# Where and when the sums of the second weight are made, and where the late weights lie

## The chip, the cores and the metric

The kernel runs on one core of one Trainium2 chip. The metric is the device time in microseconds (us) of one execution. The core has TensorE (PE; its weight loads are PEld), VectorE (DVE), ScalarE (ACT), GpSimd (POOL) and SyncE (SP), which issues the DMA transfers. Code runs on each engine in the order in which it is written; engines wait for each other through semaphores.

## The reference, cut to what matters

```
A  = softmax(q  @ k_lm^T * s)     # q, k, v: [4, 8, 576, 64]; 32 landmarks
Bm = softmax(q_lm @ k_lm^T * s);  C = softmax(q_lm @ k^T * s)
Z: six steps of Z = 2 Z - Z Bm Z
x  = (A Z C v) as tokens [2304, 512]
h  = x @ w_in;  x = (h * clip(h + 3, 0, 6) / 6) @ w_out    # FFN1, d_ff 2048
h  = x @ w_in2; g = where(h > 0, h, exp(min(h, 0)) - 1)
out = g @ w_out2                                            # FFN2, d_ff 2048
```

All data is fp32. A product on TensorE is made of pairs: each operand is split into a rounded part (hi) and the rest (lo), and three matmuls (hi hi, hi lo, lo hi) are summed. A cast on ACT makes hi, a subtraction on another engine makes lo (`to_pair`).

## The kernel before, in words

**FFN1** runs in 128 slots, 4 batches of 32. A slot has an h part (`slot_a1`) and, three slots later, the accumulation of x (`slot_a2`); the last of these are woven into FFN2's start (`late`, which the main loop takes through `tail`). Results go to DRAM as `x1d`.

**FFN2** has three tiles of 768 tokens (t = 0, 1, 2) of 8 quartets each, q = 0 to 23. A quartet (`quartet`) makes h for two d_ff blocks of 128 on each side of a seven-product form in place of eight products: seven blocks of 6 matmuls 128x384, with block sums on DVE (`a`, `u2`, `y`), then ELU on ACT and DVE (`gf`), its pair `gh`, `gl`, and one quartet later the second product (`second`, 36 matmuls 128x512 per quartet). Tile 2 (`WINO`) uses a seven-product form for the second product too (`wino2`, then `late2` for what is done after the last quartet). That form needs sums and differences of blocks of `w_out2`: `sums_out2(q)`, q = 0 to 7, reads two parts of `wo2d` (each 256 KB), makes four differences, their pairs, and stores them to `to2p` in DRAM.

**Buffers.** Tags with one buffer decide who waits. The tag `u` has three (`UB`), and is shared by the weight converters (`conv_out2`, `conv_in2`), the sums of `w_in2` in `load_in2`, the quartet's `u2`, and `sums_out2` (`scratch`; two of them, `raw` and `t`). `y` has two (`YB`). Second weights lie in four places (`w2_place`). FFN2's x of tiles 0 and 2 lies in 14 tiles `x20` to `x213` (`x_places`), that of tile 1 in the places that FFN1's weights left. `load_x(t)` loads four parts of x for each of two halves, makes seven sums of them (11 operations, with the pairs) and their casts on ACT; for tile 0 on DVE, for the others on POOL.

**Order.** The main program writes the work in the order of FFN1's slots, then of quartets with seven steps p each. `wanted(s)` gives what follows a place in time, by which the scheduler orders it on an engine against other work; `gated` holds work back to a slot. In FFN1's last batch, `sums` is stepped once a slot from slot 5 of the batch (`TSET`), and `run(sums)` does the rest before FFN2's loop. `load_x(1)` starts in q = 1 and `load_x(2)` in q = 9 (`XPACE`), a step for each p. In the last tile `late2` asks for late weight m + 3 when it starts on m, 12 of 512 KB in all:

```
if s == 0 and r % 2 == 0:
    for x in (2, 3) if m == 0 else (m + 3,):
        if x < NDEF * NQ // 2:
            load_late2(t, x)
```

Of the kernel before, what the change touches and what calls it, by code (L numbers as in the profile page):

```python
# [31 lines left out]
def nystrom_ffn_kernel(ctx: ExitStack, tc, q, k, v, w_in1, w_out1, w_in2, w_out2, out):  # L32
# [61 lines left out]
    NDEF = 3  # L94
    AHEAD = 4
# [6 lines left out]
    TSET, RUSH, LASTS = 5, 4, 4  # L102
# [272 lines left out]
    def sums_out2(q):  # L375

        raw = scratch(2, DM)
        for i in range(2):
            gated(sp.dma_start(out=raw[:, i], in_=wo2d[q + i * NQ]))
        yield  # L380
        t = scratch(4, HDM)
        (b21, b22), (b11, b12) = ((raw[:, i, 0:HDM], raw[:, i, HDM:]) for i in range(2))
        gated(sub(t[:, 0], b12, b11))
        gated(sub(t[:, 1], b22, t[:, 0]))
        gated(sub(t[:, 2], b22, b12))
        gated(sub(t[:, 3], t[:, 1], b21))
        yield
        h = raw.bitcast(F32R).rearrange("p a n -> p (a n)").rearrange("p (j n) -> p j n", j=4)
        gated(act.copy(out=h, in_=t))
        gated(sub(t.bitcast(F32R), t, h.bitcast(F32), pool))  # L390
        yield
        o = q % 2 * HDM
        for x, y in ((0, h.bitcast(F32)), (1, t)):
            sp.dma_start(out=to2p[:, q // 2, x, :, o:o + HDM].rearrange("j p n -> p j n"), in_=y)
        yield

    place = [0]
# [14 lines left out]
    def load_late2(t, m):  # L412

        j, r = (1, 2, 0)[m // (NQ // 2)], m % (NQ // 2)
        w = w2_place()
        sp.dma_start(out=w, in_=to2p[j, r].rearrange("x p n -> p x n"))
        wo2[t, "late", m] = w.bitcast(F32R)
# [561 lines left out]
    def load_x(t, eng):  # L979
# [3 lines left out]
        for kk in range(2):  # L983
# [7 lines left out]
            if t:  # L991
                f = [
                    nat.tile([128, G, HALF], F32, name="xf", tag=n).rearrange("p g t -> p (g t)")[:, 0:T2]
                    for n in ("ath0", "ath1", "atl0")
                ]
            else:
                f = [stg.tile([128, W], F32, name="xf", tag="y", bufs=YB)[:, 0:T2] for _ in range(2)]
                f.append(ft.tile([128, T2], F32, name="xf", tag="at", bufs=1))
# [175 lines left out]
    def late2(t):  # L1174
# [51 lines left out]
        for n in range(NDEF):  # L1226
# [6 lines left out]
            for r, s in order:  # L1233
# [6 lines left out]
                if s == 0 and r % 2 == 0:  # L1240
                    for x in (2, 3) if m == 0 else (m + 3,):
                        if x < NDEF * NQ // 2:
                            load_late2(t, x)
                if s == 0 and (n or r >= RUSH):
                    pair(n * NQ + r + AHEAD)
                w = wo2[t, "late", m]
                c = slice(r % 2 * HDM, r % 2 * HDM + HDM)
                for j, (g, y) in enumerate(terms(pairs[n * NQ + r], (w[:, 0, c], w[:, 1, c]))):
                    start = r == 0 and j == 0 and not (n == 0 and s == 1)
                    bmm(ps[s], g[:, tok(s)], y, start, r == NQ - 1 and j == 2 and not n == s == 0)  # L1250
                    yield
# [146 lines left out]
    def all_sums():  # L1398
        for q in range(NQ):
            yield from sums_out2(q)  # L1400

    sums = all_sums()
    for i in range(END, NA):
# [17 lines left out]
        if (i - END) % O2 == 0 and conv:  # L1421
# [3 lines left out]
            gate[0] = None  # L1425
            if not conv:
                wanted(i + 6)
                flush()
        if i >= NA - SB + TSET:
            gate[0] = marks["slot"]  # L1430
            wanted(i + 4)
            next(sums, None)
            gate[0] = None
# [23 lines left out]
    run(sums)  # L1457
# [3 lines left out]
    behind, tail, xs, n = seconds(), late(), x0, 0  # L1461
    for q in range(NTT * NQ):
# [3 lines left out]
        if q % NQ == XPACE and q // NQ + 1 < NTT:  # L1466
            xs = load_x(q // NQ + 1, pool)
        steps_ = quartet(q)
        for p in range(7):
# [5 lines left out]
            if p == 4 and q % NQ == NQ - 1 and q // NQ in WINO:  # L1475
                load_late2(q // NQ, 0)
                load_late2(q // NQ, 1)
            next(xs, None)
# [45 lines left out]
```

## Time and profile before

| | |
|---|---|
| median of 3 runs | 844.37 us (844.35 to 847.03) |
| profiled execution | 845.85 us |
| its span, first to last instruction | 844.1 us |
| its mean granted TensorE clock | 0.982 of full |
| PE, PEld busy | 786.1 (93%), 697.5 (83%) |
| DVE, ACT, POOL busy | 554.8 (66%), 463.6 (55%), 388.3 (46%) |
| DMA | 184.56 MB, mean 219 GB/s |

The profiled execution has 1.75 us around its span, and stands 1.48 over the median. FFN1 ends and FFN2 begins near 435 us; tile 1 begins near 580 and tile 2 near 707. A row of the trace gives start, duration, engine, line of the kernel, operation, out<-in by the program's names, size and count, and in square brackets the idle time just before it with what ended that. Because a helper records every operation, all rows carry the line L115; names and sizes tell operations apart. A busy PE in the trace isn't PE at its peak, so PE's clock is to be looked at with its busy time.

### The profile page before, as it was taken

To read this page: it belongs to the slowest core of one execution; us is meant where nothing else is said; L and a number is where in the kernel's file an instruction comes from. 1 tells how busy PE (TensorE), PEld (TensorE's weight loads), DVE (VectorE), ACT (ScalarE), POOL (GpSimd) and SP (SyncE) were. 2 spreads that over 40 slices of the span, in tenths; PEclk is the share of its full clock that TensorE was granted. 3 is DMA by queue.
4 is the path that set the end of the run, shared out by engine and by line. 5 is a ranking of instruction groups with operands and counts; after the bars stand their busy time and mean duration, and the time that the engine had idled before them with its cause. 6 is when DMAs were issued, how large, how long until landed. Compare 5 with 4: busy or idle time off the path is not lost.

```text
span 844.1 us, 16146 instructions
## 1 busy us (share of the span) xinstructions
PE 786.1 (93%) x5860; PEld 697.5 (83%) x5860; DVE 554.8 (66%) x1108; ACT 463.6 (55%) x1012; POOL 388.3 (46%) x383
## 2 busy tenths in 40 slices
PE   5699989999999999989993899999999999999988
PEld 3476777688878899889893799998888989999988
DVE  7898686567546654575675776655575545777774
ACT  3687545656566565664653565646544434565551
POOL 2576566557645565456667656331280000322311
PEclk9799999999999999999996999999999999999999
DMA  9966931885586546755876467686664465867455
GB/s 334 403 188 227 304 95 59 243 276 171 195 257 209 167 117 203 252 172 167 310 249 222 147 253 261 233 294 256 230 223 157 167 225 182 295 230 243 165 186 181
DMA packets 112623, 184.56 MB, mean 219 GB/s; under 512 B 8160, under 2 KB 66016, under 8 KB 112544
## 3 DMA queue, kind: packets, MB, share of 16 engines
q1 hardware_dynamic: 112544, 183.53, 64.6%
q8 instruction: 46, 0.75, 0.4%
q14 instruction: 33, 0.27, 0.1%
HBM read 130.02 MB, written 53.48 MB: 217 GB/s over the span
## 4 chain that ended last, share of the span: by engine, by line
PE 64%; DMA 11%; DVE 7%; issue 6%; POOL 6%; ACT 4%; SPq 1%; DVEq 0%; POOLq 0%; ACTq 0%
PE x L115 33%; PE h L115 26%; PE bk L115 5%; DMA u<-in_moe_w_out 3%; DVE u L115 2%; POOL gl L115 1%; DMA w<-to2p 1%; POOL x L115 1%; DMA out<-ob 1%; POOL y L115 1%; DMA wo2d<-y 1%; DMA kt<-in_k 1%; ACT u L115 1%; DMA to2p<-u 1%; DMA x<-x1d 1%
## 5 line engine op out<-in xcount | busy, mean ns | idle before, releaser
L115 PE MATMUL h<-x,wi 128*128 128x384 f32 x1008 | 206.9, 341 | 14.8 <-DVE u L115 13.2
L115 PEld LDWEIGHTS h<-x,wi 128*128 128x128 f32 x1008 | 180.1, 190 | 25.5 <-DVE u L115 14.2
L115 PE MATMUL x<-gh,wo 128*128 128x288 f32 (+1 forms) x896 | 198.8, 298 | 1.5 <-ACT xs L115 1.1
L115 PEld LDWEIGHTS x<-gh,wo 128*128 128x128 f32 x896 | 149.5, 189 | 12.1 <-issue 7.2
L115 PE MATMUL x<-gl,wo 128*128 128x288 f32 (+1 forms) x448 | 130.7, 295 | 0.6 <-POOL gl L115 0.6
L115 POOL TENSOR_TENSOR gl<-gf,gh 128x288 fp32r<-128x288 f32 (+1 forms) x100 | 85.7, 860 | 81.7 <-ACT gh L115 72.2
L115 ACT CAST gh<-gf 128x288 fp32r<-128x288 f32 (+2 forms) x160 | 72.6, 454 | 85.0 <-DVE gf L115 84.6
L115 PE MATMUL x<-w,gh 128*128 128x512 f32 (+1 forms) x420 | 114.3, 349 | 0.9 <-ACT gh L115 0.9
L115 PE MATMUL h<-atl,nh 128*128 128x288 f32 (+2 forms) x256 | 81.9, 320 | 8.6 <-DVE gf L115 5.4
L115 DVE SCALAR_TENSOR_TENSOR gf<-gf,y 128x384 f32<-128x384 f32 x80 | 59.9, 750 | 44.0 <-ACT gf L115 43.9
L115 PEld LDWEIGHTS x<-gl,wo 128*128 128x128 f32 x448 | 84.5, 189 | 2.2 <-POOL gl L115 1.1
L115 ACT ACTIVATE gf<-h,half_b 128x288 f32<-128x288 f32 (+2 forms) x128 | 63.9, 500 | 40.5 <-PE h L115 31.9
L115 POOL TENSOR_TENSOR x<-x,gf 128x384 f32<-128x384 f32 x16 | 18.2, 1158 | 145.8 <-PE x L115 86.9
L115 PE MATMUL x<-w,ghl 128*128 128x512 f32 (+1 forms) x378 | 83.9, 346 | 0.3 <-DMA w<-to2p 0.2
L115 PEld LDWEIGHTS x<-w,gh 128*128 128x128 f32 x420 | 75.3, 193 | 7.4 <-ACT gh L115 1.4
L115 DVE SCALAR_TENSOR_TENSOR gf<-gf,h 128x288 f32<-128x288 f32 (+1 forms) x112 | 49.5, 442 | 45.0 <-ACT gf L115 44.3
L115 PE MATMUL h<-ath,nl 128*128 128x288 f32 (+2 forms) x256 | 76.6, 299 | 0.0
L115 PE MATMUL h<-ath,nh 128*128 128x288 f32 (+2 forms) x256 | 76.3, 298 | 0.0
L115 PE MATMUL x<-w,gl 128*128 128x512 f32 (+1 forms) x210 | 73.6, 351 | 2.7 <-DVE gl L115 2.7
L115 ACT ACTIVATE gf<-y 128x384 f32<-128x384 f32 x80 | 42.0, 525 | 59.7 <-DVE y L115 59.7
L115 PEld LDWEIGHTS x<-w,ghl 128*128 128x128 f32 x378 | 62.1, 189 | 6.1 <-DVE ghl L115 0.4
L115 PEld LDWEIGHTS h<-atl,nh 128*128 128x128 f32 x256 | 48.4, 189 | 22.4 <-DVE gf L115 9.8
(171 smaller groups left out, 1462.1 us busy)
## 6 DMA issues: line engine op xcount, KB each, us to landing
wi<-wi2p SPq DMA_DIRECT2D x64, 448.0 KB, 5.2
wi2p<-wi SPq DMA_DIRECT2D x32, 448.0 KB, 3.1
u<-in_moe_w_in SPq DMA_DIRECT2D x25, 512.0 KB, 4.6
w1c<-w1d SPq DMA_DIRECT2D x48, 256.0 KB, 4.7
w<-wo2p SPq DMA_DIRECT2D x24, 512.0 KB, 6.3
ub<-in_moe_w_out SPq DMA_DIRECT2D x16, 512.0 KB, 10.3
u<-in_moe_w_out SPq DMA_DIRECT2D x16, 512.0 KB, 5.4
wo2p<-w SPq DMA_DIRECT2D x16, 512.0 KB, 4.0
```

Source lines behind the costliest of these rows:

```text
L115: inst = getattr(self.eng, name)(*a, **kw)
```

## The change

The sums of `w_out2` are no longer stepped in FFN1's last batch. A generator `more` steps them, one step for each p from quartet q = 8 on, so the 32 steps take q = 8 to 12. They no longer use `u`: each takes four of the x tiles `x20` to `x211`, which hold x of tile 0 before and x of tile 2 after (`spare_x`). Their four differences go from DVE to POOL; the cast of 128x1024 becomes two of 128x512, the subtraction for lo likewise, and two stores of 512 KB become four of 256 KB. Late weights 2 to 11 are loaded in halves into x tiles of tile 2, in the order in which these come free, and seven of them are asked for at m = 0; weights 0 and 1 stay in `w2_place`. x of tile 0 uses two `u` buffers where it used two `y` and one `at`. `load_x(2)` starts at q = 12 (`TX`).

```
--- before.py
+++ after.py
@@ -92,6 +92,8 @@
     WINO = (2,)
     HDM = DM // 2
     NDEF = 3
+    NLATE = 2
+    RUSH, LASTS, TX = 4, 4, 4
     AHEAD = 4
     T1 = 320
     YB, UB, SE = 2, 3, 1
@@ -99,7 +101,6 @@
     GATE1, O2, NEW1 = 8, 2, 0
     PACE, NEW, PACE1 = 0.5, -4, 0.2
     XSET, XPACE = 4, 1
-    TSET, RUSH, LASTS = 5, 4, 4
     NAT = 25, 28, 31
 
     strict = [False]
@@ -374,27 +375,28 @@
 
     def sums_out2(q):
 
-        raw = scratch(2, DM)
-        for i in range(2):
-            gated(sp.dma_start(out=raw[:, i], in_=wo2d[q + i * NQ]))
+        a, b, c, d = (spare_x(4 * q + i).rearrange("p (j n) -> p j n", j=2) for i in range(4))
+        for i, y in enumerate((b, a)):
+            sp.dma_start(out=y, in_=wo2d[q + i * NQ].rearrange("p (j n) -> p j n", j=2))
         yield
-        t = scratch(4, HDM)
-        (b21, b22), (b11, b12) = ((raw[:, i, 0:HDM], raw[:, i, HDM:]) for i in range(2))
-        gated(sub(t[:, 0], b12, b11))
-        gated(sub(t[:, 1], b22, t[:, 0]))
-        gated(sub(t[:, 2], b22, b12))
-        gated(sub(t[:, 3], t[:, 1], b21))
+        sub(c[:, 0], a[:, 1], a[:, 0], pool)
+        sub(c[:, 1], b[:, 1], c[:, 0], pool)
+        sub(d[:, 0], b[:, 1], a[:, 1], pool)
+        sub(d[:, 1], c[:, 1], b[:, 0], pool)
         yield
-        h = raw.bitcast(F32R).rearrange("p a n -> p (a n)").rearrange("p (j n) -> p j n", j=4)
-        gated(act.copy(out=h, in_=t))
-        gated(sub(t.bitcast(F32R), t, h.bitcast(F32), pool))
+        for x, y in ((a, c), (b, d)):
+            to_pair(y, x.bitcast(F32R), y.bitcast(F32R), pool)
         yield
         o = q % 2 * HDM
-        for x, y in ((0, h.bitcast(F32)), (1, t)):
-            sp.dma_start(out=to2p[:, q // 2, x, :, o:o + HDM].rearrange("j p n -> p j n"), in_=y)
+        for j, ys in enumerate(((a, c), (b, d))):
+            for x, y in enumerate(ys):
+                sp.dma_start(out=to2p[2 * j:2 * j + 2, q // 2, x, :, o:o + HDM].rearrange("j p n -> p j n"), in_=y)
         yield
 
-    place = [0]
+    def spare_x(i):
+        return xp[0].tile([128, 2, T2], F32, name="x2", tag=f"x2{i % 12}").rearrange("p a n -> p (a n)")[:, 0:2 * HDM]
+
+    place = [0, 0]
 
     def w2_place():
         place[0] += 1
@@ -412,9 +414,17 @@
     def load_late2(t, m):
 
         j, r = (1, 2, 0)[m // (NQ // 2)], m % (NQ // 2)
-        w = w2_place()
-        sp.dma_start(out=w, in_=to2p[j, r].rearrange("x p n -> p x n"))
-        wo2[t, "late", m] = w.bitcast(F32R)
+        if m < NLATE:
+            w = w2_place()
+            sp.dma_start(out=w, in_=to2p[j, r].rearrange("x p n -> p x n"))
+            wo2[t, "late", m] = [w[:, :, i * HDM:i * HDM + HDM].bitcast(F32R) for i in range(2)]
+            return
+        wo2[t, "late", m] = []
+        for i in range(2):
+            place[1] += 1
+            w = xp[0].tile([128, 2, T2], F32, name="x2", tag=f"x2{(place[1] - 1) % 14}")[:, :, 0:HDM]
+            sp.dma_start(out=w, in_=to2p[j, r, :, :, i * HDM:i * HDM + HDM].rearrange("x p n -> p x n"))
+            wo2[t, "late", m].append(w.bitcast(F32R))
 
     def load_out2(q):
 
@@ -994,8 +1004,8 @@
                     for n in ("ath0", "ath1", "atl0")
                 ]
             else:
-                f = [stg.tile([128, W], F32, name="xf", tag="y", bufs=YB)[:, 0:T2] for _ in range(2)]
-                f.append(ft.tile([128, T2], F32, name="xf", tag="at", bufs=1))
+                f = scratch(2, T2)
+                f = [f[:, 0], f[:, 1], scratch(1, T2)[:, 0]]
             for o, r, c in ((f[0], 0, 1), (l[0], 0, 0), (l[2], 1, 1), (l[1], 1, 0)):
                 sp.dma_start(out=o, in_=x1d[2 * r + kk, :, t0 + c * T2:t0 + c * T2 + T2])
             yield
@@ -1238,14 +1248,13 @@
                     if r == RUSH:
                         inline()
                 if s == 0 and r % 2 == 0:
-                    for x in (2, 3) if m == 0 else (m + 3,):
+                    for x in range(2, 9) if m == 0 else (m + 6,) if m > 2 else ():
                         if x < NDEF * NQ // 2:
                             load_late2(t, x)
                 if s == 0 and (n or r >= RUSH):
                     pair(n * NQ + r + AHEAD)
-                w = wo2[t, "late", m]
-                c = slice(r % 2 * HDM, r % 2 * HDM + HDM)
-                for j, (g, y) in enumerate(terms(pairs[n * NQ + r], (w[:, 0, c], w[:, 1, c]))):
+                w = wo2[t, "late", m][r % 2]
+                for j, (g, y) in enumerate(terms(pairs[n * NQ + r], (w[:, 0], w[:, 1]))):
                     start = r == 0 and j == 0 and not (n == 0 and s == 1)
                     bmm(ps[s], g[:, tok(s)], y, start, r == NQ - 1 and j == 2 and not n == s == 0)
                     yield
@@ -1395,11 +1404,6 @@
     newton(2)
     conv = [lambda kk=kk: conv_out2(kk) for kk in range(NKT)]
     conv += [lambda m=m, kk=kk: conv_in2(m, kk) for m in range(NQ) for kk in range(2)]
-    def all_sums():
-        for q in range(NQ):
-            yield from sums_out2(q)
-
-    sums = all_sums()
     for i in range(END, NA):
         b, r = i // SB, i % SB
 
@@ -1423,14 +1427,6 @@
             wanted(i + 4)
             conv.pop(0)()
             gate[0] = None
-            if not conv:
-                wanted(i + 6)
-                flush()
-        if i >= NA - SB + TSET:
-            gate[0] = marks["slot"]
-            wanted(i + 4)
-            next(sums, None)
-            gate[0] = None
         if i >= NA - SB + XSET:
             wanted(i + 4)
             next(x0, None)
@@ -1454,18 +1450,19 @@
         for q in range(NTT * NQ):
             yield from (wino2 if q // NQ in WINO else second)(q)
 
-    run(sums)
     flush()
     wanted(NA - 6)
     load_in2(1)
-    behind, tail, xs, n = seconds(), late(), x0, 0
+    behind, tail, xs, more, n = seconds(), late(), x0, iter(()), 0
     for q in range(NTT * NQ):
         wanted(NA + 4 * q - 2)
         if q:
             load_in2(q + 1) if q + 1 < NTT * NQ else None
-        if q % NQ == XPACE and q // NQ + 1 < NTT:
+        if q % NQ == (TX if q // NQ + 1 in WINO else XPACE) and q // NQ + 1 < NTT:
             xs = load_x(q // NQ + 1, pool)
         steps_ = quartet(q)
+        if q == (WINO[0] - 1) * NQ:
+            more = (None for r in range(NQ) for _ in sums_out2(r))
         for p in range(7):
             if p == 2:
                 load_out2(q)
@@ -1475,6 +1472,7 @@
             if p == 4 and q % NQ == NQ - 1 and q // NQ in WINO:
                 load_late2(q // NQ, 0)
                 load_late2(q // NQ, 1)
+            next(more, None)
             next(xs, None)
             wanted(NA + 4 * q + 4 * p / 7)
             next(steps_)
```

**DVE, where FFN1 ends and FFN2 begins.** `gf` and `gl` of 128x288 are FFN1's; `u<-u 128x256` are differences of the second weight; `u<-u,wi` and `u<-wi,u` are `load_in2(1)`'s sums; rows with `a_` are quartet 0's, `u<-h,a_` its `u2`. Before:

```order
L115 SCALAR_TENSOR_TENSOR gf<-gf,h 128x288
L115 TENSOR_TENSOR u<-u 128x256 x3
L115 TENSOR_TENSOR gl<-gf,gh 128x288
L115 TENSOR_TENSOR u<-u 128x256
L115 TENSOR_TENSOR y<-h,a_5917 128x384
L115 SCALAR_TENSOR_TENSOR gf<-gf,y 128x384
L115 TENSOR_TENSOR gl<-gf,gh 128x384
L115 TENSOR_TENSOR u<-u 128x256 x4
L115 TENSOR_TENSOR u<-u,wi 128x128 x2
L115 TENSOR_TENSOR u<-wi,u 128x128 x2
L115 TENSOR_TENSOR u<-h,a_5917 128x384
L115 TENSOR_TENSOR u<-u,wi 128x128
L115 TENSOR_TENSOR u_5919<-h,u 128x384
```

After the change:

```order
L116 TENSOR_TENSOR gl<-gf,gh 128x288
L116 SCALAR_TENSOR_TENSOR gf<-gf,h 128x288
L116 TENSOR_TENSOR gl<-gf,gh 128x288
L116 TENSOR_TENSOR u<-h,a_5819 128x384
L116 TENSOR_TENSOR y<-h,a_5819 128x384
L116 TENSOR_TENSOR u_5821<-h,u 128x384
L116 SCALAR_TENSOR_TENSOR gf<-gf,y 128x384
L116 TENSOR_TENSOR gl<-gf,gh 128x384
L116 TENSOR_TENSOR y<-h,u_5821 128x384
L116 TENSOR_TENSOR u<-h,u 128x384
L116 TENSOR_TENSOR y<-h,u_5821 128x384
L116 SCALAR_TENSOR_TENSOR gf<-gf,y 128x384
```

The eight differences of the second weight are gone, the sums of quartet 1's weight no longer stand here (two and two of them now stand 12 to 18 rows higher, between FFN1's `gf` and `gl`, and the others behind quartet 0's next rows), and quartet 0's `u2` stands ahead of its first `y`.

**ACT, in quartet 0 and at quartet 1's first block.** `COPY a_` opens quartet 1; `CAST x_` are casts of x of tile 1, `CAST gh` make the pair of quartet 0's ELU. Before:

```order
L115 CAST x_6403<-xf 128x384
L115 ACTIVATE gf<-gf 128x384
L115 ACTIVATE gf<-y 128x384
L115 COPY a_6115<-h 128x384
L115 CAST wi<-wi 128x384
L115 ACTIVATE gf<-gf 128x384
L115 CAST gh<-gf 128x384
```

After the change:

```order
L116 CAST gh<-gf 128x384
L116 ACTIVATE gf<-gf 128x384
L116 COPY a_6017<-h 128x384
L116 CAST x_6303<-xf 128x384
L116 ACTIVATE gf<-y 128x384
L116 CAST wi<-wi 128x384
L116 CAST gh<-gf 128x384
```

A cast of x of tile 1 stood ahead of `a` and the ELU's rows; it now stands between `a` and the second of the two `gh` casts.

**SP, the last weight loads.** `w_` are in `w2_place`, `x_` in x tiles, `to2p` are late weights, `wo2p` the last quartet's. Before:

```order
L115 DMA w_9626<-wo2p 128x2x512
L115 DMA w_9664<-to2p 128x2x512
L115 DMA w_9666<-to2p 128x2x512
L115 DMA w_9777<-to2p 128x2x512
L115 DMA w_9806<-to2p 128x2x512
L115 DMA w_9871<-to2p 128x2x512
L115 DMA out<-ob 128x256 x2
L115 DMA w_9779<-to2p 128x2x512
L115 DMA out<-ob 128x256
L115 DMA w_9899<-to2p 128x2x512
L115 DMA w_9936<-to2p 128x2x512
L115 DMA w_9963<-to2p 128x2x512
```

After the change:

```order
L116 DMA x_9823<-to2p 128x2x256
L116 DMA x_9837<-to2p 128x2x256
L116 DMA w_9672<-wo2p 128x2x512
L116 DMA x_9831<-to2p 128x2x256
L116 DMA x_9845<-to2p 128x2x256
L116 DMA x_9825<-to2p 128x2x256
L116 DMA x_9839<-to2p 128x2x256
L116 DMA x_9833<-to2p 128x2x256
L116 DMA x_9847<-to2p 128x2x256
L116 DMA x_9829<-to2p 128x2x256
L116 DMA x_9843<-to2p 128x2x256
L116 DMA w_9710<-to2p 128x2x512
```

Ten late halves now stand ahead of weight 0 (`w_9710`), where before weights 0 and 1 came first and each next one when a place came free.

## Rows read from the trace of the kernel before

**Rows 1.** Windows: span, busy us of each engine, clock, DMA share, GB/s

```profile
core 0: us, PE busy (x) PEld busy (x) DVE busy (x) ACT busy (x) POOL busy (x), PEclk, DMA share, GB/s
440.00:460.00 20.00, 6.25 (x30) 5.78 (x30) 10.16 (x21) 6.21 (x11) 15.46 (x12) 0.71 0.54 187
```

**Rows 2.** Chain that ended last, part of the join: start, us, what

```profile
446.41 2.69 DVE u L115 x3
...
454.00 2.18 POOL wi L115 x2
456.19 0.57 DVE u L115
```

**Rows 3.** Timeline of PE at the join: start, us, engine, what, idle before

```profile
435.23 1.21 PE L115 MATMUL h<-x,wi 128*128 128x384 f32 x6
436.28 0.29 PE L115 MATMUL x<-gh,wo 128*128 128x288 f32 x1
...
437.07 1.22 PE L115 MATMUL h<-x,wi 128*128 128x384 f32 x6
...
456.80 1.65 PE L115 MATMUL h<-x,wi 128*128 128x384 f32 x4 [12.91 <-DVE u L115]
...
472.38 0.79 PE L115 MATMUL x<-w,gl 128*128 128x512 f32 x1 [2.74 <-DVE gl L115]
...
483.88 1.23 PE L115 MATMUL h<-x,wi 128*128 128x384 f32 x6
484.94 0.62 PE L115 MATMUL x<-w,gh 128*128 128x512 f32 x2
...
486.31 0.87 PE L115 MATMUL h<-x,wi 128*128 128x384 f32 x4
```

**Rows 4.** Timelines of POOL and SP at the join

```profile
434.02 1.01 POOL L115 TENSOR_TENSOR xf<-xf,x 128x384 f32<-128x384 f32 x1 [0.64 <-PE h L115]
...
459.06 1.01 POOL L115 TENSOR_TENSOR xf<-xf,x 128x384 f32<-128x384 f32 x1
...
455.01 0.48 SPq L115 DMA_DIRECT2D xf<-x1d  x1
```

**Rows 5.** Timelines in FFN1's last slots: PE, POOL, DVE

```profile
379.70 0.40 PE L115 MATMUL h<-atl,nh 128*128 128x288 f32 x1 [1.40 <-DVE gf L115]
...
406.62 0.40 PE L115 MATMUL h<-atl,nh 128*128 128x288 f32 x1 [1.39 <-DVE gf L115]
...
402.67 2.38 POOL L115 TENSOR_TENSOR u<-u 128x1024 fp32r<-128x1024 f32 x1 [2.62 <-ACT u L115]
...
403.09 2.91 DVE L115 TENSOR_TENSOR u<-u,wi 128x128 f32<-128x128 f32 x2 [1.27 <-DMA u<-wi2d]
405.93 0.28 DVE L115 TENSOR_TENSOR u<-wi,u 128x128 f32<-128x128 f32 x1
```

**Rows 6.** Timeline of PE near the end

```profile
818.87 3.04 PE L115 MATMUL h<-w,ghl 128*128 128x256 f32 x18 [3.42 <-DMA w<-to2p]
...
823.63 0.45 PE L115 MATMUL x<-w,gh 128*128 128x256 f32 x2
...
827.99 3.40 PE L115 MATMUL x<-w,ghl 128*128 128x256 f32 x27
```

**Rows 7.** Groups of instructions by shape: count, busy us, mean ns, idle before

```profile
L115 POOL TENSOR_TENSOR gl<-gf,gh 128x256 fp32r<-128x256 f32 x16 | 12.0, 748 | 9.2 <-ACT gh L115 9.2
...
L115 POOL TENSOR_TENSOR wi<-u,wi 128x512 fp32r<-128x512 f32 x16 | 21.1, 1333 | 0.0
...
L115 POOL TENSOR_TENSOR x<-xf,x 128x384 fp32r<-128x384 f32 x16 | 18.4, 1160 | 0.0
...
L115 ACT CAST x<-xf 128x384 fp32r<-128x384 f32 x24 | 12.1, 511 | 13.0 <-POOL xf L115 8.4 <-DVE xf L115 4.4
```

**Rows 8.** Windows of tile 1: columns as in the first group

```profile
608.00:624.00 16.00, 15.68 (x78) 13.75 (x77) 10.07 (x13) 7.93 (x18) 13.43 (x13) 1.00 0.56 194
624.00:640.00 16.00, 15.28 (x76) 13.43 (x75) 11.13 (x18) 8.79 (x19) 10.31 (x9) 1.00 0.55 182
640.00:656.00 16.00, 16.00 (x81) 14.35 (x80) 8.45 (x16) 6.90 (x14) 0.00 (x0) 1.00 0.51 180
```

**Rows 9.** The page's DMA queues: packets, MB, share of 16 engines' span

```profile
q1 hardware_dynamic: 112544, 183.53, 64.6%
```

## The prediction, made before the changed kernel ran

> **What bounds the kernel now.** I read the time in windows first, then the chain of work that ended last, then TensorE's own instructions around every wait. PE is busy 93% of the span, so only places where PE stands still, or runs at the lower clock, are worth anything. In 440 to 460 us PE works 6.25 of 20 us at a mean granted clock of 0.71, while POOL is busy 15.46 [rows 1]. It is the largest gap of the trace, and it lies at the join of the two FFNs. The chain through it [rows 2] has no PE: DVE `u` work (2.69), later POOL `wi` (2.18), then DVE `u` again (0.57). The first are sums of the second weight (they hold two of the three `u` buffers), the last is quartet 0's own `u2`, which can only have a buffer when sums and the weight load of quartet 1 have given theirs back. PE's rows there show one wait of 12.91 on DVE `u` and one of 2.74 on `gl` [rows 3]. Two smaller places count: two stalls of 1.40 and 1.39 in FFN1's last slots [rows 5], and 3.42 at the very end, on a late weight from `to2p` [rows 6].
>
> **Term 1, the join.** From quartet 0's block 0 (435.23) to quartet 2's (483.88) is 48.65 us [rows 3]. The work in it at full speed: 14 h blocks of 1.05 (435.23 to 436.28), 36 FFN1 matmuls of 0.132 (six from 436.28 to 437.07) and 30 second matmuls of 0.228 (six from 484.94 to 486.31): 14.7 + 4.75 + 6.85 = 26.3. So 22.4 are lost now, in waits and in the lower clock behind them. The change takes all sums out of the `u` buffers here, so half of quartet 1's weight sums stand 14 rows ahead of quartet 0's `u2` on DVE in place of right before it, the other half behind it, and `u2` has its buffer at once; the row order of DVE at the join shows it. What is late next is x of tile 1, which stays where it was: its first half starts on POOL at 434.02 [rows 4]; 11 operations of 1.16 [rows 7] end at 446.8. The second half's load takes from SP 455.01 to POOL 459.06, 4.05 [rows 4], so 450.9, and its first POOL operation (1.01) ends at 451.9. On ACT, in the order after the change, a cast of `x` stands between quartet 0's two `gh` casts; cast, relu, `wi` cast, `gh` cast at about 0.51 each (the form 128x384) [rows 7] end at 453.9. PE would need that `gh` at 435.23 + 7.35 + 4.75 + 2.1 (two more blocks) + 0.7 (three second matmuls) = 450.1. That leaves 3.8 idle, and about 1.5 of lower clock behind it, taken from the late stage: 27 matmuls took 4.76 (818.87 to 823.63) behind a 3.42 wait where 27 take 3.24 normally (3.40 less the last one's tail) [rows 6]. 22.4 - 5.2 = **-17.2**. Bounds: -20.6 if the cast of x comes without idling PE for long, and -12.0 if waits of 10 us stay.
>
> **Term 2, FFN1's last slots.** The eight 128x1024 subtractions on POOL leave. At 402.67 one of 2.38 runs beside a pair of 128x128 subtractions on DVE that take 2.91 (two more of the kind take 0.28 each right behind them), and PE then waits 1.39 [rows 5]; the other wait, 1.40, stands behind such an operation too. I take both off: **-2.8**. Bounds: 0 (x of tile 0 now needs two `u` buffers, and may bring waits of its own) to -4.5 (the smaller ones go too).
>
> **Term 3, the late weights.** Ten of twelve now have a place of their own from the freed x tiles, and the first seven of these are asked for together, long before use. The 3.42 wait and 1.5 behind it [rows 6] go; I keep 0.6, as weights 0 and 1 are still asked for behind other loads on SP. **-4.3**; bounds -1.5 (a first weight is as late as now by half) to -5.3.
>
> **Term 4, the middle tile.** Eight sums in 32 steps, seven a quartet: 4.6 quartets. A quartet is 7 x 1.05 + 36 x 0.228 = 15.6 us by rows 3, so 72 us. POOL gets 8 x (4 subtractions of 128x256 at 0.75 + 2 of 128x512 at 1.33) = 45 us [rows 7], ACT 16 casts 128x512, some 0.65 each scaled from 0.51. POOL is idle there now and ACT 40% busy. But POOL's work isn't free for the others: in 608 to 640, where POOL makes x of tile 2 (13.43 + 10.31 = 23.7 us), PE was idle 0.32 + 0.72 = 1.04, and in 640 to 656, without POOL, not at all [rows 8]. In proportion, 45 x 1.04 / 23.7 = **+2.0**; bounds 0 (quartets have slack at every other place) to +5.8 (three times that, since the operations come in one order with the casts). x of tile 2 starts three quartets later and meets the last sums; its last cast still stands at quartet 15's start, one quartet ahead of use, so I cost it at nothing; without that cover it would cost some 5 us once.
>
> DMA moves the same bytes in smaller parts: 32 stores of 256 KB for 16 of 512 KB, and 20 late halves for 10 whole weights. SP issues 26 more, which the quartets' PE time hides as it hides the others; without that cover each would cost about what the 0.48 of SP's row is [rows 4], 12 us.
>
> **Sum.** -17.2 - 2.8 - 4.3 + 2.0 = -22.3. The profiled run took 845.85, so 823.5; it stood 1.48 over the median of 844.37, so I forecast **822.0** us.
>
> **The rivals.**
> *The join keeps more.* With the `u` wait gone, x of tile 1 or the load of quartet 1's weights is late by 10 us more than worked out: term 1 falls to about -7, 832 us. For it: POOL is at 15.46 of 20 us there [rows 1]; against it: 2 x 2.4 of that are sums that leave.
> *DMA fills up.* Sums read and write 12.6 MB in 72 us. 183.53 MB take 64.6% of 844.1 [rows 9], so 12.6 MB take 37 us, +0.52 on a share of 0.51 to 0.56 [rows 8]: full. Then weights of quartets 9 to 12 come late; they are asked for a quartet ahead, so I give +5, 827 us.
> *DVE is blocked by POOL.* If each DVE operation with two SBUF inputs, of which a quartet has 8, waited for a whole POOL operation (as the pair at 403.09 did [rows 5]), DVE would need 8.45 [rows 8] + 8 x 1.31 = 18.9 us for a quartet of 15.7: 3.2 x 4.6 = +15, 837 us in all. Against it: POOL is busy 62% of that stretch, not all, and an operation met at its middle costs half, so 8 x 0.62 x 0.65 = 3.3 us, 11.7 in all, under 15.7. The Trainium skill, "SBUF — State Buffer", section "Who interferes with whom", says that a DVE instruction with two SBUF inputs and a GpSimd instruction share a port pair which one of them locks until it is done; by that rule alone, with every operation hit, it is this rival. The trace agrees on the single case: 2.91 for two operations of 0.28 beside POOL's 2.38.
> *Slower than before.* ACT runs in order, and its 16 casts stand behind POOL's subtractions. The x places turn every third sums: load 4, subtractions 3.0, casts 1.3, subtractions 2.7, store 4, some 15 us against 27 (three times four steps of 2.24). If that chain is over 27 us (loads waiting behind others on a full DMA), casts hold ACT, `gf` and `gh` of the quartet come late, and PE stands. From about 3 us over at each sums it costs 8 x 3 = 24 and more, ending at 847 or above. Against it: the slack of 12 us.
> *It doesn't do it*: another holder of the `u` buffers takes the place of the sums (x of tile 0 takes two of three), the 12.91 stays: 842 to 846.
>
> **How the numbers follow.** Forecast (814 to 826) 0.68; join keeps more 0.10; DMA full 0.08; DVE blocked 0.06; slower 0.05; no effect 0.03. About 0.3%, 2.5 us, is what a measurement of this kernel can tell from no change. With every term at its best bound the sum is -20.6 - 4.5 - 5.3 + 0 = -30.4, or 814.0 by the median; half of the way there is 818. With every term at its worst it is -12.0 + 0 - 1.5 + 5.8 = -7.7, or 836.7. The range takes the whole of the first, since small waits that I didn't price may go too, and of the second up to the DMA case and the join rival: 814 to 832. Slower 0.05, the same 0.02, faster the rest, 0.93.
>
> **What would show it.** Right: PE's wait on DVE `u` at the join gone or under 5 us, the first wait there on ACT `gh` or `gl`, near quartet 1's second block; 440 to 460 with over 14 us of PE; no 1.4 us waits on `gf` in 365 to 410; no PE wait on `to2p` over 1 us at the end; POOL busy near 45 us more from quartet 8 to 12, with 1 to 4 us of PE idle. Wrong: PE waits on ACT `gh` or on `xs` in quartets 8 to 12 that add up to more than 6, DVE operations beside POOL's subtractions at over 1 us each, a DMA share at 1.0 there, or a wait of 10 us at the join under another name.

## The result and the profile after

| | before | after |
|---|---|---|
| median | 845.67 us (4 runs, 844.35 to 847.03) | 821.87 us (4 runs, 820.59 to 825.72) |
| ratio | 1 | 0.9726 (95%: 0.9686 to 0.9766) |
| profiled run, its span | 845.85, 844.1 | 820.95, 819.2 |
| PE busy | 786.1 (93%) | 783.4 (96%) |

The time lies at the forecast (822.0), 2.7% under the kernel before. Run again later, beside other kernels, the changed kernel took 821.41 (819.47 to 822.85). In the profiled run 24.9 us of span have gone. Where, is seen from points of the program that both traces have. First the join, as a window of 440 to 460 us in the profile after:

```profile
core 0: us, PE busy (x) PEld busy (x) DVE busy (x) ACT busy (x) POOL busy (x), PEclk, DMA share, GB/s
440.00:460.00 20.00, 14.83 (x68) 12.92 (x67) 15.59 (x24) 10.35 (x23) 16.24 (x14) 0.91 0.37 127
```

PE works 14.83 us where it worked 6.25 [rows 1], at a clock of 0.91 against 0.71. PE's timeline after, from quartet 0's first block to quartet 2's:

```profile
428.89 1.23 PE L116 MATMUL h<-x,wi 128*128 128x384 f32 x6
...
445.48 0.73 PE L116 MATMUL x<-w,gh 128*128 128x512 f32 x2 [1.45 <-ACT gh L116]
...
450.98 0.68 PE L116 MATMUL x<-w,gl 128*128 128x512 f32 x1 [3.72 <-DVE gl L116]
...
462.61 1.23 PE L116 MATMUL h<-x,wi 128*128 128x384 f32 x6
```

The wait of 12.91 on DVE `u` [rows 3] is gone; two others, 1.45 and 3.72, are left. The stretch took 48.65 and takes 33.72. What ends the 3.72 stands in DVE's timeline:

```profile
444.56 2.01 DVE L116 TENSOR_TENSOR u<-u,wi 128x128 f32<-128x128 f32 x2 [0.98 <-POOL xf L116]
446.49 1.10 DVE L116 TENSOR_TENSOR u<-wi,u 128x128 f32<-128x128 f32 x1
447.51 1.07 DVE L116 TENSOR_TENSOR u<-u,wi 128x128 f32<-128x128 f32 x1
448.51 0.55 DVE L116 TENSOR_TENSOR u<-h,a 128x384 f32<-128x384 f32 x1
...
449.58 1.35 DVE L116 TENSOR_TENSOR gl<-gf,gh 128x384 fp32r<-128x384 f32 x1
```

`gf` and `gh` of this `gl` were done at 443.6 and 445.4, but seven weight sums and `u2` stand in front of it, four of the seven at 1.0 us in place of 0.28, beside POOL's x of tile 1. They are quartet 2's sums: a quartet has eight, and DVE had done quartet 0's by 374 and quartet 1's by 415. The prediction, and the order of rows that it read, took them for the second half of quartet 1's.

In FFN1's last slots, PE's waits from 365 to 412:

```profile
PE h L116 <- DVE gf L116: 1.4, 2, 0.8
```

The two of 1.4 [rows 5] have gone. In the middle tile, where the sums run now, PE shows no wait at all from 540 to 700. These are windows of quartets 8 to 11:

```profile
556.00:572.00 16.00, 16.00 (x80) 14.14 (x80) 10.12 (x16) 10.50 (x22) 14.62 (x14) 1.00 1.02 353
572.00:588.00 16.00, 16.00 (x81) 14.40 (x80) 12.80 (x19) 9.28 (x19) 12.66 (x12) 1.00 1.06 384
588.00:604.00 16.00, 16.00 (x81) 14.37 (x80) 9.95 (x18) 8.55 (x17) 5.81 (x6) 1.00 1.06 375
604.00:620.00 16.00, 16.00 (x82) 14.44 (x81) 8.65 (x15) 7.91 (x17) 11.53 (x12) 1.00 1.06 391
```

PE is busy 16.00 of 16 throughout, with a DMA share of 1.02 to 1.06, which means that all 16 DMA engines are full. At the end one late weight is still waited for (before: 3.42 [rows 6]):

```profile
787.88 0.51 PE L116 MATMUL h<-w,gh 128*128 128x256 f32 x2 [1.74 <-DMA w<-to2p]
```

For all kernels of this study, here are four stretches between such points, in us of the profiled execution. S1 runs from one wait on `gf` in FFN1's last batch (at 360.27 before, 358.41 after) to quartet 0's first block; S2 from there to the `COPY a<-h` of quartet 2; S3 from there to that of quartet 16; S4 from that of quartet 23 to the end of the span. In e5 PE doesn't wait at S1's point, so it has none.

| kernel | reached S1 | S1 | S2 | S3 | S4 | median of runs |
|---|---|---|---|---|---|---|
| before | 360.27 | 74.96 | 51.56 | 219.86 | 51.24 | 845.67 |
| after | 358.41 | 70.48 | 36.27 | 218.66 | 49.18 | 821.87 |
| after, again (e12) | 361.84 | 70.48 | 35.87 | 219.47 | 47.14 | 821.41 |
| e1 | 362.58 | 70.50 | 41.73 | 223.86 | 47.13 | 834.42 |
| e2 | 360.26 | 72.36 | 36.23 | 220.02 | 47.13 | 824.93 |
| e3 | 359.86 | 70.52 | 36.18 | 220.73 | 51.21 | 826.93 |
| e4 (of before) | 361.85 | 75.08 | 52.59 | 219.34 | 51.84 | 846.88 |
| e5 | none | none | 36.78 | 219.62 | 47.21 | 822.91 |
| e6 | 363.26 | 70.51 | 35.27 | 229.19 | 48.84 | 827.07 |
| e7 | 361.74 | 70.69 | 36.30 | 223.11 | 47.36 | 825.97 |
| e8 | 361.80 | 70.52 | 34.08 | 219.38 | 45.42 | 818.88 |
| e9 | 361.30 | 70.48 | 31.50 | 229.12 | 46.50 | 826.47 |
| e10 | 359.71 | 70.47 | 28.40 | 230.65 | 45.48 | 823.43 |
| e11 | 360.14 | 70.59 | 35.71 | 221.80 | 46.86 | 825.13 |

The time at which S1 is reached varies from 358.4 to 363.3; for the changed kernel alone, in its two profiles, by 3.4. So medians that differ by 2 or 3 us say little. In the same two profiles S1, S2 and S3 agree to 0.0, 0.4 and 0.8 us and S4 to 2.0, so small effects are read from the stretches. The three rows of each that the columns S2 to S4 rest on are, for the changed kernel, ACT's:

```profile
465.16 0.48 ACT L116 COPY a<-h 128x384 f32<-128x384 f32 x1
...
683.82 0.48 ACT L116 COPY a<-h 128x384 f32<-128x384 f32 x1 [0.53 <-PE h L116]
...
770.02 0.48 ACT L116 COPY a<-h 128x384 f32<-128x384 f32 x1
```

ACT's copy can come late after its block on PE, so here are PE's own points too, the start of the first h block of quartets 0, 2 and 16:

| kernel | quartet 0 | quartet 2 | quartet 16 | 0 to 2 | 2 to 16 |
|---|---|---|---|---|---|
| before | 435.23 | 483.88 | 705.41 | 48.65 | 221.53 |
| after | 428.89 | 462.61 | 682.58 | 33.72 | 219.97 |
| e12 | 432.32 | 465.42 | 686.42 | 33.10 | 221.00 |
| e1 | 433.08 | 471.29 | 697.43 | 38.21 | 226.14 |
| e6 | 433.77 | 466.90 | 694.51 | 33.13 | 227.61 |
| e7 | 432.43 | 466.85 | 690.60 | 34.42 | 223.75 |
| e8 | 432.32 | 461.99 | 684.54 | 29.67 | 222.55 |
| e9 | 431.78 | 459.54 | 691.16 | 27.76 | 231.62 |
| e10 | 430.18 | 456.62 | 687.98 | 26.44 | 231.36 |
| e11 | 430.73 | 463.86 | 687.00 | 33.13 | 223.14 |

### The profile page after: what moved, and what is told of

Same layout as the page of the kernel before. It is cut to its first block, busy times and chain, and to the rows that moved or that the text cites. A ratio compares the mean times of both kernels' runs of the same rounds, so it can differ in the third digit from the quotient of the medians.

```text
span 819.2 us, 16236 instructions
## 1 busy us (share of the span) xinstructions
PE 783.4 (96%) x5860; PEld 696.6 (85%) x5860; DVE 541.0 (66%) x1076; ACT 465.1 (57%) x1020; POOL 415.2 (51%) x423
## 4 chain that ended last, share of the span: by engine, by line
PE 75%; DVE 10%; DMA 9%; ACT 2%; issue 2%; POOL 1%; SPq 0%; DVEq 0%; ACTq 0%; POOLq 0%
PE x L116 39%; PE h L116 31%; PE bk L116 5%; DMA u<-in_moe_w_out 2%; DMA u<-in_moe_w_in 2%; DVE u L116 2%; DVE h L116 1%; DMA kt<-in_k 1%; DMA w1d<-w1c 1%; DVE w1c L116 1%; DVE nl L116 1%; DMA w<-to2p 1%; DVE lm L116 1%; DVE st L116 1%; DVE gf L116 1%
## 5 line engine op out<-in xcount | busy, mean ns | idle before, releaser
L116 POOL TENSOR_TENSOR gl<-gf,gh 128x288 fp32r<-128x288 f32 (+1 forms) x100 | 83.3, 835 | 86.4 <-ACT gh L116 78.9
L116 PE MATMUL x<-w,gh 128*128 128x512 f32 (+1 forms) x360 | 102.5, 358 | 1.4 <-ACT gh L116 1.4
L116 DVE SCALAR_TENSOR_TENSOR gf<-gf,y 128x384 f32<-128x384 f32 x80 | 64.1, 801 | 32.5 <-ACT gf L116 32.5
L116 PE MATMUL x<-w,ghl 128*128 128x512 f32 (+1 forms) x324 | 77.2, 359 | 0.1
L116 PEld LDWEIGHTS x<-w,gh 128*128 128x128 f32 x360 | 65.1, 190 | 7.9 <-ACT gh L116 1.9
L116 PE MATMUL x<-w,gl 128*128 128x512 f32 (+1 forms) x180 | 64.6, 359 | 3.7 <-DVE gl L116 3.7
L116 PEld LDWEIGHTS x<-w,ghl 128*128 128x128 f32 x324 | 56.0, 192 | 5.8 <-DVE ghl L116 0.3
```

The lines of the kernel that those rows point to most:

```text
L116: inst = getattr(self.eng, name)(*a, **kw)
```

## The experiments

**e1 and e2: what about the sums cost the join?** The theory is that the last sums hold two of three `u` buffers. In the trace before, DVE stood idle for 5.55 us in front of quartet 0's `u2`, whose inputs don't come from POOL, until POOL had done with a sum of quartet 1's weight, which is in a `u` buffer:

```profile
456.19 0.56 DVE L115 TENSOR_TENSOR u<-h,a 128x384 f32<-128x384 f32 x1 [5.55 <-POOL wi L115]
```

The rival is that the sums' work, wherever it is in FFN1's last batch, costs PE time.

```
-more = (None for r in range(NQ) for _ in sums_out2(r))
+more = (None for r in range(NQ) if r not in QS for _ in sums_out2(r))
 # and in FFN1's last batch, as the kernel before does it, in u buffers:
+if i >= NA - SB + SLOT: next(old, None)     # old: sums of r in QS
 # e1: QS = (6, 7), SLOT = 29;  e2: QS = (0, 1), SLOT = 5
```

> Changed kernel, but sums 6 and 7 are made again in u buffers at the end of FFN1, as before; the other six stay in the middle tile. Buffer theory: what cost the join was that the last sums hold two of three u buffers, so quartet 0's u2 waits; two sums are enough for that, PE waits on DVE u for 9 us or more again, 831 to 836 us (the changed kernel took 821.9). Rival, work theory: it was the sums' DVE and POOL work, which shares out over all eight; two of eight give back 14.9 x 2/8 = 3.7, 825.6 us.

> Changed kernel, but sums 0 and 1 are made again in u buffers, from slot 5 of FFN1's last batch, far from the join; the other six stay in the middle tile. Buffer theory: the join stays as in the changed kernel, at most 2 us come back from stalls on gf beside POOL's 128x1024 subtractions, 822 to 824 us. Work theory: the same 3.7 us as for the last two, 825.6 us.

Measured: e1 834.42 us (831.04 to 834.85), e2 824.93 (822.43 to 826.29). PE's waits in e1 from 433 to 490:

```profile
PE h L116 <- DVE u L116: 6.1, 3, 2.9
PE h L116 <- DVE y L116: 2.9, 1, 2.9
PE h L116 <- DVE gf L116: 1.5, 1, 1.5
PE x L116 <- DVE ghl L116: 0.4, 1, 0.4
```

The wait on `u` is back, in three parts of up to 2.9 and not as one of 9; S2 and S3 are 5.5 and 4 to 5 us longer, which is 10 of the 12.5 us by which the median of e1 is longer. Two sums far from the join cost 1.9 in S1 and nothing in S2; e2's median lies between the two forecasts. So it is where they stand, and the work theory (825.6 for both) falls by e1. That it is their buffers is less clear. The row above shows it in the kernel before, for 5.55 of the 12.91 us. In e1 `u2` stands right behind quartet 1's weight sums on DVE, and no idle time on a buffer is in front of it. No run puts the sums' work at the join into other buffers, so what their work costs there by itself stays open.

**e3: the late weights as before.**

```
-for x in range(2, 9) if m == 0 else (m + 6,) if m > 2 else ():
+for x in (2, 3) if m == 0 else (m + 3,):
 # and all 12 in w2_place
```

> Changed kernel, but all twelve late weights go through the four places again, asked for three ahead. The prediction's term: 4.3 us, 826.2. From the two traces, from quartet 23 to the end: 2.1 us, 824.0, as the changed kernel still waits 1.74 for weight 1. If the term is nothing: 821.9.

Measured: 826.93 us (825.93 to 828.98), with 3.02 of waiting where the changed kernel's two profiles have 1.74 and 1.25:

```profile
799.12 1.20 PE L116 MATMUL h<-w,ghl 128*128 128x256 f32 x4 [3.02 <-DMA w<-to2p]
```

S4 is 51.21, as before the change, against 47.14 in e12 and 47 in most others. The profile after, with 49.18, and e6, with 48.84, are the odd ones: behind the wait of 1.74 in the profile after, the window 786 to 802 has a granted clock of 0.89, and in e12, behind one of 1.25, 1.00. So the term is 4.1 us in most executions, near the prediction's 4.3, and the 2.1 of the first two traces came of an execution with the lower clock.

**e4: x of tile 2 later, alone, in the kernel before.**

```
-if q % NQ == XPACE and q // NQ + 1 < NTT:
+if q % NQ == (4 if q // NQ + 1 in WINO else XPACE) and q // NQ + 1 < NTT:
```

> Kernel before, with one edit: x of tile 2 is made from quartet 12 on and not from 9. Theory that the stalls of 1.04 in quartets 10 and 11 belong to where this work stands: they go, and 1.0 to 1.6 us of 845.7, 844.1 to 844.7. Rival, that they belong to POOL's work as such, as the prediction's fourth term has it: the stalls move along, 845.7.

Measured: 846.88 us, ratio 1.0016 (0.9989 to 1.0042): the same. S3 is 219.34, and 219.86 before. But the edit didn't move the work. These are the rows at which POOL starts on x of tile 2, before and in e4:

```profile
606.57 1.01 POOL L115 TENSOR_TENSOR xf<-xf,x 128x384 f32<-128x384 f32 x1 [32.30 <-DMA xf<-x1d]
...
608.39 1.42 POOL L115 TENSOR_TENSOR xf<-xf,x 128x384 f32<-128x384 f32 x1 [31.51 <-ACT gf L115]
```

PE starts on quartet 8 at 577.99 and at 580.60, so POOL starts 28.6 and 27.8 us behind that, and in both it is done before 637. The stall of 0.68 on `y` in quartet 11 is still there, beside the same work. So e4 settles neither reading. What does bear on it is the changed kernel, where x of tile 2 has moved, to 633 to 673: PE has no wait there, in the first profile and in e12.

**e5: x of tile 0 in its old buffers.**

```
-f = scratch(2, T2)
-f = [f[:, 0], f[:, 1], scratch(1, T2)[:, 0]]
+f = [stg.tile([128, W], F32, name="xf", tag="y", bufs=YB)[:, 0:T2] for _ in range(2)]
+f.append(ft.tile([128, T2], F32, name="xf", tag="at", bufs=1))
```

> Changed kernel, but x of tile 0 is made in two y buffers and one at buffer as before, not in two u. The prediction gives this edit no term of its own. If the u buffers that it takes delay anything, the time falls to 820 or under; if the y buffers and at were what it waited for in FFN1's last slots (y is what the converters and the first ELU use), the time rises by 1 to 4 us, 823 to 826; nothing: 821.9.

Measured: 822.91 us (820.45 to 825.61), and S2 to S4 as in the changed kernel. Nothing is seen of it there, as forecast by leaving it out; S1, where it would act first, has no point to measure from.

**e6, e11 and e7: what the middle tile can carry.** e6 repeats POOL's four differences three times, e11 twice (a loop around them); e7 takes `pool` off them, so that DVE makes them.

> Changed kernel, but POOL makes the four differences of each of the eight sums three times over (the result is the same), 64 operations of 128x256 more, at 0.75 to 1.1 us each 48 to 70 us more of POOL in quartets 7 to 12. Prediction's fourth term, 1.04 us of PE idle for 23.7 us of POOL: +2.1 to +3.1, 824 to 825. Theory from the trace after (PE never waits there, DVE has slack): below +0.5, 821.9 to 822.4. Slower-side rival of the prediction, the chain of a sums passes its room of 27 us: +20 and more.

> Changed kernel, POOL makes the four differences of each sums twice (32 operations of 128x256 more, some 28 us). Three times cost 9 to 10 us between quartet 2 and 16. If the cost goes with POOL's time: half, 5 us, 825 to 827. If it begins where POOL is full for whole quartets (it was at 16.0 of 16 there with three): 0 to 1.5, 822 to 823.5, with POOL under 15 of 16 us in most of the stretch.

> Changed kernel, but the four differences of each sums are made on DVE and not on POOL, still in the middle tile. DVE is busy 9 to 12 of 16 us there and POOL was idle before; 32 operations of 0.38 are 12 us over 72. Theory that DVE's order matters only where a wait ends on it: same as the changed kernel, 821.5 to 822.5. Port rival of the prediction (POOL's subtractions lock out DVE): the time falls by a part of what they cost, 820 to 821.

Measured: e6 827.07 us (825.84 to 832.66), e11 825.13 (823.10 to 827.13), e7 825.97 (823.12 to 827.16). S3 is 229.19, 221.80 and 223.11, against 218.7 to 220.7 in kernels with the change's own middle tile. In e6, 2.5 us of that are ACT's copy of quartet 16 alone, which stands that much further behind its block on PE than elsewhere (698.23 against 694.51; after, 683.82 against 682.58). By PE's blocks of quartets 2 and 16, against e12, the three cost 6.6, 2.1 and 2.8 us. By medians, against 821.41 to 821.87, it is 5.2 to 5.7, 3.3 to 3.7 and 4.1 to 4.6; e6's profile is of an execution of 832.66 us, 5.6 over its median. Three times doesn't give the 0 that the trace after suggested, nor the 2 to 3 of the prediction's proportion. Windows of e6:

```profile
572.00:588.00 16.00, 14.73 (x70) 11.98 (x69) 9.45 (x15) 7.68 (x16) 16.00 (x20) 1.00 0.80 271
...
620.00:636.00 16.00, 15.03 (x73) 12.63 (x71) 10.66 (x15) 7.34 (x15) 16.00 (x18) 1.00 0.59 194
```

POOL is full (16.00 of 16), and PE stands for about 1 in 16. In e11 PE has waits of 1.36, 0.77 and 0.17 us; POOL is at 16.00 and 15.92 in the two windows around the first, and at 13.70 in the window of the other two. By POOL's rows by shape the eight sums take 50 us in the changed kernel, 78 in e11 and 105 in e6. So the price isn't in proportion to all of POOL's work: the first 50 us cost nothing (S3 219.5 in the middle against 219.86 and 219.34 without sums there). Of the rest, 28 us cost 2 to 4 and 55 us 5 to 7. Whether the second half costs more than the first isn't settled: by PE's blocks twice costs a third of what three times does, by medians some two thirds, and e11's median lies in the range of the proportional reading. "Begins where POOL is full" isn't shown: e11's POOL isn't under 15 in its first windows as that theory asked, and e6's PE is busy 16.00 of 16 in 604 to 620 beside a POOL at 15.84. What slows down is seen in DVE's operations by shape. First the kernel before, 644 to 705, with POOL idle:

```profile
L115 DVE SCALAR_TENSOR_TENSOR gf<-gf,y 128x384 f32<-128x384 f32 x15 | 8.4, 559 | 10.7 <-ACT gf L115 10.7
L115 DVE TENSOR_TENSOR y<-h,u 128x384 f32<-128x384 f32 x12 | 6.7, 558 | 4.1 <-PE h L115 4.1
L115 DVE TENSOR_TENSOR gl<-gf,gh 128x384 fp32r<-128x384 f32 x10 | 5.6, 558 | 2.5 <-ACT gh L115 1.9
```

The changed kernel, 556 to 620:

```profile
L116 DVE SCALAR_TENSOR_TENSOR gf<-gf,y 128x384 f32<-128x384 f32 x17 | 12.5, 738 | 6.5 <-ACT gf L116 6.5
L116 DVE TENSOR_TENSOR gl<-gf,gh 128x384 fp32r<-128x384 f32 x10 | 8.6, 862 | 3.2 <-ACT gh L116 2.8
L116 DVE TENSOR_TENSOR y<-h,u 128x384 f32<-128x384 f32 x13 | 7.2, 553 | 2.0 <-PE h L116 2.0
```

And e6, 556 to 652:

```profile
L116 DVE SCALAR_TENSOR_TENSOR gf<-gf,y 128x384 f32<-128x384 f32 x23 | 22.3, 970 | 13.6 <-ACT gf L116 13.6
L116 DVE TENSOR_TENSOR gl<-gf,gh 128x384 fp32r<-128x384 f32 x15 | 15.7, 1046 | 10.2 <-ACT gh L116 9.8
L116 DVE TENSOR_TENSOR y<-h,u 128x384 f32<-128x384 f32 x18 | 9.8, 546 | 1.4 <-PE h L116 1.4
```

`gf` and `gl`, with both inputs in SBUF, go from 0.56 to 0.74 and 0.86 and then to 0.97 and 1.05; `y<-h,u`, whose `h` comes from a PSUM bank, stays at 0.55. This is the rival of a DVE blocked by POOL, in its place but at a fraction of its price. That DVE has the room for it in the changed kernel, and that in e6 the chain of a quartet's ELU no longer fits, is a reading of these rows; no run isolates it. In e7 the four differences are back on DVE, which is busy 14.45 and 14.24 of 16 in 556 to 572 and 572 to 588, and PE waits 1.73 on `y` right behind that, at 589. So their move to POOL is worth some 3 to 4 us of what the middle tile could have cost.

**e8, e9 and e10: what is left at the join and at the end.** e8 puts quartet 2's weight sums (first DVE sum, first ACT cast) behind quartet 0's last pair, and gives late weights 0 to 6 and 11 the x tiles in the order in which quartet 23 frees them, 7 to 10 the four places. e9 is the changed kernel with x of tile 1 behind quartet 1's pairs. e10 has all three.

```
 # e8, join: in load_in2, for q == 2 (after: an order, no wait)
+after(first_sum, last_gl); after(first_cast, last_gh)
 # e8, late weights
-w = xp[0].tile(..., tag=f"x2{(place[1] - 1) % 14}")
+x = (0, 7, 4, 11, 1, 8, 5, 12, 3, 10, 6, 13, 2, 9)[(place[1] - 1) % 14]
+w = xp[0].tile(..., tag=f"x2{x}")
 # e9: XPACE = 2, and in load_x for t == 1
+after(first_sub, last_gl)
```

> Changed kernel with two edits. At the join, quartet 2's weight sums on DVE and their cast on ACT stand behind quartet 0's last gl and gh, which they held up by 3.7 us. At the end, late weights 0 to 6 take x tiles in the order in which the last quartet frees them and 7 to 10 the four places, so that no weight is asked for behind another that waits. Theory: both waits go with the low clock behind them: up to 5 at the join, 3 at the end, 814 to 818. Rival: the join's wait comes from x of tile 1 on POOL and returns under another name, only the end's gain stays: 819.

> Changed kernel, with x of tile 1 made on POOL and cast on ACT only behind quartet 1's pairs, so that neither POOL nor ACT has it at the join. The prediction's theory of what is left at the join (its x of tile 1, late on POOL, holds the cast of gh on ACT): the waits of 1.45 on gh and 3.72 on gl go with some clock, 816 to 818 us. Rival, from the trace after (quartet 2's weight sums stand in front of gl on DVE): they run faster without POOL beside them, 0.28 each in place of 1.0, so the gl wait shrinks by 2 to 3 but stays, 818.5 to 820. If x of tile 1 is then late for tile 1, PE waits at quartet 8 and the time is over 822.

> The three edits together: quartet 2's weight sums behind quartet 0's last pair, x of tile 1 behind quartet 1's pairs, late weights in the order in which their tiles come free. If each takes a wait of its own: 813 to 816 us, and under 2 us of PE idle from quartet 0 to 2. If the first two take the same wait: as with two edits, 817 to 819.

Measured: e8 818.88 us (817.71 to 821.24), e9 826.47 (824.13 to 828.79), e10 823.43 (822.63 to 826.97). e8 is the fastest of all (ratio to before 0.9676, 0.9634 to 0.9718). It takes 1.7 off S4, where no wait on a weight is left. It takes 1.8 to 2.2 off S2 (3.4 to 4.1 by PE's blocks, of which 1.5 or more come back behind quartet 2's start), less than the 5 expected, since part of the join's wait returns under another name, as its rival said. PE's waits in e8 from 430 to 475:

```profile
PE h L116 <- DVE u L116: 2.8, 2, 1.7
PE x L116 <- ACT gh L116: 0.6, 1, 0.6
PE h L116 <- ACT ghl L116: 0.2, 1, 0.2
```

e9 takes 4.4 to 4.8 off S2 and e10 7.5 to 7.9; by PE's blocks it is 5.3 to 6.0 and 6.7 to 7.3. e10's join is free of waits. e9's has one of 0.73 left, on the same `gl`, with quartet 2's sums still in front of it on DVE:

```profile
446.06 0.62 DVE L116 TENSOR_TENSOR u<-u,wi 128x128 f32<-128x128 f32 x2 [0.42 <-issue]
...
448.07 1.37 DVE L116 TENSOR_TENSOR gl<-gf,gh 128x384 fp32r<-128x384 f32 x1
...
449.49 0.50 PE L116 MATMUL x<-w,gl 128*128 128x512 f32 x1 [0.73 <-DVE gl L116]
```

The seven sums and `u2` take 2.0 us there, where they took 5.0 beside POOL's x of tile 1, as e9's rival said. So x of tile 1 holds most of the join by making quartet 2's sums long, and their place on DVE by itself is worth 1.3 more (27.76 to 26.44). The two edits overlap and don't add up: 3.4 to 4.1 and 5.3 to 6.0 alone, 6.7 to 7.3 together. But S3 is 9.7 to 11.2 longer. PE's waits in e9 from 460 to 545:

```profile
PE h L116 <- DVE u L116: 5.3, 3, 2.9
PE x L116 <- DVE gl L116: 0.9, 1, 0.9
```

x of tile 1 now meets the weight pairs of quartets 3 to 6 on POOL (13.59, 14.42 and 14.12 of 16 us in the windows from 462 to 510), DVE's weight sums slow down beside it, and `u2` of the quartet is late. The work isn't late for its tile, which was the failure that was expected; it costs where it is made. No run found a place in tile 0 where it is free.

**e12: the changed kernel again.**

> The changed kernel itself, once more, beside the other three. The same time as before, 821.9 within some 2 us; its trace shows what of the waits is the same from run to run: 1 to 1.5 on gh and 3.4 to 3.8 on gl at the join, 1.2 to 1.8 on a late weight.

Measured: 821.41 us, with 0.97 on `gh`, 3.57 on `gl`, 1.25 on a late weight, and 0.57 on `u` in quartet 8, which the first profile didn't have. As expected but for the 0.97.

## Why the prediction was right

The time and its sign were right, and so were the places and the directions of terms 1 to 3. One term was very near, the others were off by about 2 us each, not all the same way. Measured by the stretches of the profiles:

| term | predicted | measured |
|---|---|---|
| 1, the join | -17.2 | -14.9 to -15.6 by PE's blocks (48.65 to 33.72, 33.10); -15.3 to -15.7 by S2 (51.56 to 36.27, 35.87) |
| 2, FFN1's last slots | -2.8 | -4.5 (S1, 74.96 to 70.48) |
| 3, late weights | -4.3 | -4.1 (S4, 51.24 to 47.14) |
| 4, middle tile | +2.0 | 0 to -1.6 (S3, 219.86 to 218.66 and 219.47; PE's blocks, 221.53 to 219.97 and 221.00) |
| sum | -22.3 | -23.9 with -15.3 and 0 (medians: -23.8) |

**Term 1** had the right place and the right cause, the last sums at the join (e1, e2); their `u` buffers are shown by the trace before for a part of it. Of what is left, 6.8 to 7.4 us by PE's blocks where 5.2 were expected (3.8 + 1.5, which is 5.3), the two waits stand where it said, at second matmuls in quartet 1 on `gh` and `gl`. The wait on `gh` is the one it worked out, and was sized too large, 1.45 and 0.97 where it had 3.8. The wait on `gl`, 3.72 and 3.57, is not in its sum. It comes from x of tile 1 on POOL, which makes quartet 2's sums ahead of `gl` long on DVE (e9), where the prediction had x of tile 1 delay only ACT's casts. **Term 2** was too small: it counted the two large stalls, and its own outer bound, -4.5, in which the small ones go too, is what came. That is more than the waits show: those that PE has in S1 fall from 4.5 us to 1.4, with 0.6 and 0.8 on `gf` left, and where the other 1.4 us come from isn't shown. **Term 3** was right in size, though the 0.6 that it kept for weights asked for behind others was a wait of 1.74 with a lower clock behind it in the profile after, and of 1.25 at full clock in e12; e8's order takes it away.

**Term 4** is the step that failed. It took PE's idle time beside POOL's x of tile 2, 1.04 for 23.7, as a rate per us of POOL, where the sums' 50 us of POOL (45 forecast) cost nothing: PE's waits from 540 to 700 went from 1.0 to 0, and to 0.57 in e12. The rate failed for its own source too, as x of tile 2, in its new place from 633 to 673, stops PE nowhere. What the runs put in its place is a price that starts only behind the first 50 us (e6, e11). Why it starts there is argued from DVE's rows and not shown.

The terms' errors, +1.9, -1.7, +0.2 and -2.0, leave -1.6 in all. The forecast also started from a median of 844.37, and that of four runs is 845.67, 1.3 higher. The two nearly cancel, so that the forecast lies 0.1 us from the median is luck of that size.

Of its signs of being right, two didn't come: PE did wait over 1 us on `to2p`, and had no idle time of 1 to 4 us in quartets 8 to 12. Of its signs of being wrong, two came without a cost: the DMA share over 1.0, and single DVE operations over 1 us beside POOL (up to 1.64).

**The rivals.** The join kept 2 us more, not 10. DMA did fill up, as worked out (1.03 forecast, 1.02 to 1.06 seen), but PE never waited for a weight there: asking a quartet ahead was enough, so the step from "full" to 5 us didn't follow. POOL did slow DVE's operations with two SBUF inputs, but by 0.2 to 0.3 us each in the mean and not by 1.3. The slower side and no effect were not seen.

## What to carry to other kernels

Where one tag with few buffers is shared by many small jobs, look at what stands at a change of stage and who holds the tag there: putting two jobs of eight back at the join cost 10 us in the stretches around it, and two others, far from it, cost 2. Work moved onto an idle engine can be free only up to a point, here perhaps set by the slack of the engine that it slows down, so double it and triple it before calling it free or pricing it by the us. Before a run counts for or against a reading, look in its trace whether the edit moved the work at all (e4), and read a stretch from the engine that matters, not from another that can lag behind it (e6). And a job that costs at one place may cost more at the next (e9): measure the stretch behind the one that is mended.

## What the runs showed of the hardware that was not expected

Only DVE operations with both inputs in SBUF grew beside POOL (0.56 to 0.86 and 1.05 us), none that reads PSUM (0.55 in all three). The Trainium skill, "SBUF — State Buffer", section "Who interferes with whom", has the rule that a DVE instruction with at most one SBUF input, "outside the 2-port perf modes", does not contend with GpSimd, and one with two does when the GpSimd instruction reads SBUF. The rows agree.

All 16 DMA engines were at 1.02 to 1.06 for 64 us, at 353 to 391 GB/s, while PE never waited in that execution. Here a full DMA was no bound, with weights asked for a quartet, 15.6 us, ahead.

A wait of 1.74 near the end left PE at a mean clock of 0.89 for the window behind it, and one of 1.25 at the same place, in another execution of the same kernel, at 1.00. S4 differs by 2.0 us between the two, of which 0.5 are the waits themselves: behind a wait of this size the lower clock cost nearly as much as the wait in one execution, and nothing in the other.
